# A spectral filter and a squared-ReLU MLP in one kernel: first part reordered, one residual by matmul, two column stages ahead in the drain, bias adds moved

## The chip, the cores and the metric

The kernel runs on one core of a Trainium2 chip. The core has five instruction queues that run side by side[...]: TensorE (PE, matrix multiplies, which write PSUM), VectorE (DVE), ScalarE (ACT), GpSimd (POOL) and SyncE (SP, which issues loads and stores). The metric is device time in microseconds (us) of one launch. A chunk of work is faster only if the last instruction of the program ends earlier, so what matters is who waits for whom.

## The reference, cut to what matters

Both halves work on x of 2048 rows and 512 columns, in bf16, and both have a residual.

```python
h  = x + irfft2(rfft2(layernorm(x)) * (w_r + 1j * w_i))     # w: 2048 x 257
u  = layernorm(h)
a  = relu(u @ w1 + b1) ** 2                                 # w1: 512 x 1792
out = h + a @ w2 + b2                                       # w2: 1792 x 512
```

The Fourier transforms are done as matrix products with tables of sines and cosines. The layernorm has no gain or bias; its mean only touches one frequency column, so the first part needs just the reciprocal standard deviation of each row.

## The kernel before, in words

**Layout.** Row 16p + g of x lies in partition p, group g, so there are 16 groups of 128 rows (tile xs).

**First part (to L315).** Pool makes index tables by iota and memset (L136 to L157). DVE turns them into angles (L159 to L178): fiE[0] (L168) for the table EF of the row transform, fiK (L172, L174) for the table KF. ACT takes sines of them (L191 to L194). Pool makes fiE[1] (L179) and the angles fiG of the column transform (`angles_g`, L181). Meanwhile each group's variance is found: bn_stats and bn_aggr on DVE (`ln1_stats`, L204), for groups 3, 7 and 11 two activations with sums on ACT (`ln1_sums`, L197). Pool turns a variance into the reciprocal deviation rs1 with an add and a power (`ln1_rstd`, L215), and DVE scales the table KF by it into KFr (`ln1_fold`, L219). `stage1` (L223) then multiplies two groups of x by KFr on PE, eight matmuls of 256 columns, and copies the result to Bt. With split=True the two halves of the result lie in two PSUM tiles, and ACT and DVE copy one each. `warm` (L248) issues filler matmuls on a tile of ones, which compute nothing that is used.

SP's queue issues the loads in this order: five pieces of x, then the two filter arrays w_r and w_i (WB, L102), W1, W2, b1, b2 (L103 to L106). Two gathers with reversed row order (`w_reversed`, L148) are issued by Pool (L300, L301). ident, the identity matrix for transposes, is made by Pool (L296, L297).

**Middle (L318 to L470).** The spectrum is worked on in eight pairs of row frequencies, pr = 0 to 7. `stage2` is the column transform (PE, then a copy to U), `stage3` the row transform (PE, then a copy to X, or to AB with a butterfly on DVE for odd pr), `spectral` (L390) the filter on DVE: two products mA and mB, their combination Z, and M, the sums and differences of Z that the next stage takes. `stage4` (L413) is the inverse row transform: PE, then a copy to T2. The inverse tables EI and KI are transposes of EF and KF (`transposed`, L253; `table_i`, L260; `table_neg`, L265). The loop at L448 issues, in each turn, stage2 of pr + 3, stage3 of pr + 2, stage4 of pr - 1 and spectral of pr. All stages draw PSUM from four tiles of two banks. The sine of the last table GI is taken at pr = 4 (L467), the table of the square root is loaded at pr = 8 (L470).

**Drain (L660 to L674).** `s5` is the inverse column transform of one group: four matmuls, and a copy od of one half by ACT. `s5b` makes the sum and difference R on DVE. `s6` multiplies by KI and adds the residual x on DVE, giving hs. `s6b` gives mean and variance, either by two activations on ACT or by bn_stats on DVE. `rstd`, `norm` and `transp` give the normalised, transposed input UT of the MLP. In the drain this is done for chunk 0 (groups 0 and 1); nothing else can run on PE meanwhile, so `warm` fills it.

**MLP (L588 on).** The 16 groups go in chunks of 2, 3, 4, 4 and 3. For each chunk come 14 up slots (four matmuls into ph, a ReLU on ACT into rl, a square on DVE into act) and, for each group, three down slots (5, 5 and 4 matmuls into po), then the output: DVE adds hb, which is hs + b2, made on Pool (L605), and SP stores it. The column stages of the next chunk are placed between these slots by `prep_steps` (L564) and `run` (L645): each step has a due time in estimated PE time, and is issued after the slot at which the running sum of estimates (0.22 us for each matmul of 512 columns, 0.44 for an s5, 0.12 for each group of a transpose step) has reached it. What is still left is issued after the last slot. PSUM has 3 banks for pp, 3 for ph, 2 for po.

At the end `pin` (L22) fixes the program order of each engine as it was written. Semaphore waits and the reuse of buffers follow from the data.

The order of the first part, as it stands before, in short:

```python
    ln1_stats(0, 1); ln1_rstd(0, 2); angles_g(0)
    ln1_stats(2, 4, 5); ln1_fold(0, 2); stage1(0, 8)
    ln1_rstd(2, 6); angles_g(1)
    ln1_stats(6, 8, 9); ln1_fold(2, 6); stage1(2)
```

Of the kernel before, what the change touches and what calls it, by code (L numbers as in the profile page):

```python
# [15 lines left out]
P = 128  # L16
# [18 lines left out]
def kernel(  # L35
# [38 lines left out]
    ident = persist.tile([P, P], BF16, name="ident")  # L74
    mhalf = persist.tile([P, 4], FP32, name="mhalf")
# [9 lines left out]
    WB = [fwd.tile([P, 23, Df], BF16, name=f"WB{i}") for i in range(2)]  # L85
# [5 lines left out]
    Cn = fwd.tile([P, len(ON_PE), P], BF16, name="Cn")  # L91
    KFr = fwd.tile([P, G, 256], BF16, name="KFr")
# [4 lines left out]

    CH = ((0, 2), (2, 4), (4, 8), (8, 12), (12, 16))
    for a, b in CH:
        nc.sync.dma_start(xs[:, a:b, :], xv[:, a:b, :])  # L100
    for i in range(2):
        nc.sync.dma_start(WB[i][:, 0:16, :], wvs[i])  # L102
    nc.sync.dma_start(W1[:], B_w1.rearrange("(c p) f -> p c f", p=P))  # L103
    nc.sync.dma_start(W2[:], B_w2.rearrange("(i p) d -> p i d", p=P))
    nc.sync.dma_start(b1b[:], B_b1.rearrange("(i p) -> p i", p=P))
    nc.sync.dma_start(b2b[:], B_b2.unsqueeze(0).to_broadcast([P, D]))  # L106
# [37 lines left out]
    nc.gpsimd.iota(subc[:], pattern=[[0, 16], [1, 8]], base=0, channel_multiplier=0)  # L144
    nc.gpsimd.iota(idxR[:], pattern=[[0, 1]], base=(P - 1) * 16 * 257, channel_multiplier=-16 * 257)
    nc.gpsimd.memset(ones[:], 1.0)  # L146

    def w_reversed(i):  # L148
        nc.gpsimd.indirect_dma_start(
            out=WB[i][:, 16:23, :].rearrange("p j l -> p (j l)"), out_offset=None,  # L150
            in_=(A_w_r, A_w_i)[i].rearrange("k l -> (k l)").unsqueeze(1), element_offset=9 * Df,
            in_offset=bass.IndirectOffsetOnAxis(ap=idxR[:, 0:1], axis=0))
# [4 lines left out]
    nc.gpsimd.memset(eps[:], EPS)  # L157

# [15 lines left out]
    nc.vector.scalar_tensor_tensor(fiK[:], subc[:].rearrange("p q s -> p (q s)"), pF[:, 2:3], fiK[:],  # L174
                                   ALU.is_equal, ALU.mult)

    nc.vector.tensor_scalar(cols[:, 0:1], pF[:, 0:1], 128.0, None, ALU.mult)
    nc.vector.tensor_scalar(cols[:, 1:2], pF[:, 0:1], 128.0, 16384.0, ALU.mult, ALU.add)  # L178
    nc.gpsimd.tensor_scalar(fiE[1][:], fiE[0][:], 1.0, float(QT), ALU.mult, ALU.add)  # L179
# [14 lines left out]
    table_e(1)  # L194
# [28 lines left out]
    def stage1(g0, n=0, split=False, cp=nc.scalar.copy):  # L223
# [7 lines left out]
        warm(pts[0], n)  # L231
        for t in range(2):
# [8 lines left out]
        if split:  # L241
            for t, cp in ((0, nc.scalar.copy), (1, nc.vector.tensor_copy)):
                cp(dst[:, 2 * t:2 * t + 2], pts[t].rearrange("p (e i q s) -> p e i q s", e=2, i=2, q=16))
            return two[0][:, 512:1024].bitcast(BF16)
        else:
            cp(dst, pt[:].rearrange("p (e i q s) -> p e i q s", e=4, i=2, q=16))
# [21 lines left out]
    for g in (3, 7, 11):  # L268
        ln1_sums(g)
    ln1_stats(0, 1)  # L270
    ln1_rstd(0, 2)
    angles_g(0)
    ln1_stats(2, 4, 5)
    ln1_fold(0, 2)
    stage1(0, 8)
    ln1_rstd(2, 6)
    angles_g(1)
    ln1_stats(6, 8, 9)
    ln1_fold(2, 6)
    stage1(2)  # L280
    ln1_rstd(6, 10)
    stage1(4)
    ln1_stats(10, 12)
    ln1_rstd(10, 12)
    ln1_fold(6, 10)
    stage1(6)
    ln1_stats(13)
    ln1_fold(10, 12)
    ln1_rstd(12, 14)
    sin_of(GF[:].rearrange("p t c -> p (t c)"), fiG[:])  # L290
    stage1(8)
    ln1_stats(14, 15)
    ln1_rstd(14, 16)
    ln1_fold(12, 14)
    stage1(10, cp=nc.vector.tensor_copy)
    nc.gpsimd.memset(ident[:], 0.0)  # L296
    nc.gpsimd.affine_select(out=ident[:], in_=ident[:], compare_op=ALU.not_equal,  # L297
                            fill=1.0, base=0, pattern=[[-1, P]], channel_multiplier=1)
    ln1_fold(14, 16)
    w_reversed(0)  # L300
    w_reversed(1)  # L301
    stage1(12, split=True)
    tr08 = stage1(14, split=True)
# [3 lines left out]
    nc.vector.tensor_scalar(Cn[:], EF[:, ON_PE[0]:ON_PE[-1] + 1:ON_PE[1] - ON_PE[0], 1, :], -1.0, None, ALU.mult)  # L307
    transposed(tr08, (0, 8), True)
# [7 lines left out]


# [3 lines left out]
    def stage2(pr, split=False):  # L321
        Us[pr] = U = fwd.tile([P, 2, 512], BF16, tag="U", bufs=3, name="U")
        if split:
            pus = [mm_tile(f"p2{q}")[:, 0:512] for q in range(2)]
        else:
            pu = mm_tile("p2")
            pus = [pu[:, 0:512], pu[:, 512:1024]]
        for q in range(2):
            puv = pus[q].rearrange("p (r e j) -> p r e j", r=2, e=2)
            for e in range(2):  # L330
                for t in range(2):
                    nc.tensor.matmul(puv[:, :, e, :], lhsT=Bt[:, 2 * t + 1 - e, 2 * pr + q, :], rhs=GFv[:, t, :, e, :],  # L332
                                     start=(t == 0), stop=(t == 1))
        Uv = U[:].rearrange("p q (r j e) -> p (q r) j e", r=2, e=2)
        if split:
            for q, cp in ((0, nc.scalar.copy), (1, nc.vector.tensor_copy)):
                cp(Uv[:, 2 * q:2 * q + 2], pus[q].rearrange("p (r e j) -> p r j e", r=2, e=2))
        else:
            nc.scalar.copy(Uv, pu[:].rearrange("p (q r e j) -> p (q r) j e", q=2, r=2, e=2))  # L339
# [49 lines left out]
    def spectral(pr):  # L389
# [4 lines left out]
        step = 23 - 2 * pr if pr else 8  # L394
# [3 lines left out]
        Ms[pr] = M = fwd.tile([P, 2, 2, 256], BF16, tag="M", bufs=2, name="M")  # L398
        ABs.pop(pr, None)
        nxt[0]()  # L400
        nc.vector.tensor_tensor(Z[:, :, 0], mA[:, :, 0], mB[:, :, 1], ALU.subtract)
        nc.vector.tensor_tensor(Z[:, :, 1], mA[:, :, 1], mB[:, :, 0], ALU.add)
        nxt[1]()
        if pr == 0:
            nc.vector.tensor_scalar(M[:, :, 0], Z[:, :, 1], -1.0, None, ALU.mult)
            nc.vector.tensor_copy(M[:, :, 1], Z[:, :, 0])
        else:
# [5 lines left out]
    def stage4(pr, split=False):  # L413
        Z, M = Zs.pop(pr), Ms.pop(pr)
        pts = [mm_tile("p4a"), mm_tile("p4b")] if split else [mm_tile("p4")] * 2
        for lt in (1, 0, 3, 2):
            r, e = lt // 2, lt % 2
            pt = pts[r]
            if pr == 0:
                for u, k1 in ((0, 0), (1, 8)):  # L420
                    o = pt[:, 256 * lt + P * u:256 * lt + P * u + P]
                    nc.tensor.matmul(o, lhsT=Z[:, u, r, e::2], rhs=EI[:, k1, 1, :], start=True, stop=False)
                    nc.tensor.matmul(o, lhsT=M[:, u, r, e::2], rhs=EI[:, k1, 0, :], start=False, stop=True)
            else:
                o = pt[:, 256 * lt:256 * lt + 256]
                ei = EI[:, pr].rearrange("p k b -> p (k b)")
# [10 lines left out]
    stage2(0, split=True)  # L437
    stage2(1)
    stage3(0)
    nc.scalar.copy(KI[:], tr08[:, 4 * P:5 * P])  # L440
    table_i(tr08, (0, 8))
# [6 lines left out]
    for pr in range(9):  # L448
        if pr + 3 < 8:
            stage2(pr + 3)  # L450
        if 0 < pr and pr + 2 < 8:
            stage3(pr + 2)
        if pr > 0:
            stage4(pr - 1, split=(pr == 8))
        if pr >= 5:
            warm(mm_tile("idle")[:, 0:512], 5)
        if pr < 8:
            spectral(pr)
        if pr == 0:
            table_neg((1, 3))  # L460
# [29 lines left out]
    def s5(g):  # L490
        pe = bank("p5", "pp", 3)
# [5 lines left out]
        od = ffn.tile([P, 256], FP32, tag="od", bufs=3, name="od")  # L497
# [9 lines left out]
    def s6(g):  # L507
        py = bank("p6", "pp", 3)
        nc.tensor.matmul(py[:], lhsT=KI[:], rhs=Rs.pop(g)[:], start=True, stop=True)  # L509
        nc.vector.scalar_tensor_tensor(hs[:, g, :], py[:], WSC, xs[:, g, :], ALU.mult, ALU.add)  # L510
# [16 lines left out]
    def rstd(c):  # L527
        a, b = CHUNKS[c]
        for par in range(2):
            mine = [g for g in range(a, b) if on_act(c, g) != bool(par)]  # L530
            if mine:
                st = mine[1] - mine[0] if len(mine) > 1 else 1
                sl = slice(mine[0], mine[-1] + 1, st)
                nc.scalar.activation(sd2[:, sl], mv2[:, sl, 1], ACT.Sqrt, bias=eps[:], scale=1.0 if par else 1.0 / D)
# [29 lines left out]
    def prep_steps(c, total):  # L564
# [3 lines left out]
        t0 = 0.3 if c == 1 else total - 0.5 - 2.0 * n - 7.0  # L568
# [139 lines left out]
```

## Time and profile before

| | us |
|---|---|
| median of 4 runs | 179.16 (178.15 to 179.37) |
| the profiled execution | 178.93 |
| its span, first to last instruction | 177.1 |
| granted TensorE clock, mean | 0.979 of full |
| PE busy | 161.7 (91%) |
| DVE busy | 129.1 (73%) |
| ACT busy | 105.9 (60%) |
| POOL busy | 37.0 (21%) |

All times of instructions below are from the start of the span. L12 is line 12 of the kernel before. The first part lasts to about 21.7, the middle to 53.7 (the first s5), the drain to 61.0 (the first matmul of the MLP), the first MLP chunk to 76.9, the other four to 174.0, where the last output is added and stored. A busy PE counts matmuls whose ends are modelled, so the distance between the starts of two matmuls says more than their length. In the chain of waits each row is what the end of the program depended on at that moment.

### The profile page before, as it was taken

Reading aid. Unit: us, or ns where it says so; the run is one execution under the profiler, and the core shown is the slowest. Engines: PE = TensorE matmul, PEld = TensorE weight load, DVE = VectorE, ACT = ScalarE, POOL = GpSimd, SP = SyncE. Lnnn points to the kernel's source line nnn. Section 1 sums busy time; section 2 is a strip of 40 time slices with the busy share of each in tenths; the row PEclk is TensorE's granted clock in tenths of the full one; section 3 lists DMA queues with packets and bytes.
Section 4 is the critical chain, followed back from the end, with each engine's and each line's share of the span. In section 5 each row is a group of like instructions: output and inputs, shape, how many; then the busy total and the mean of one; then the engine's idle time right before and its main releaser. Section 6 shows DMA issues by size and latency. Waiting matters only on the chain.

```text
span 177.1 us, 2715 instructions
## 1 busy us (share of the span) xinstructions
PE 161.7 (91%) x984; PEld 93.0 (52%) x984; DVE 129.1 (73%) x300; ACT 105.9 (60%) x184; POOL 37.0 (21%) x62
## 2 busy tenths in 40 slices
PE   3479898999888899999999999999999999999992
PEld 1157566777453576466544544544544454455461
DVE  6999779799976479869889466579756648468321
ACT  3976677998845586059753488454278623568300
POOL 7585841000000050006100053100025200025000
PEclk9956999999999999999999999999999999999999
DMA  5999992000000000010000100000100000110011
GB/s 148 331 408 417 359 319 41 0 4 2 0 0 0 4 2 0 0 61 4 0 0 31 60 1 0 2 30 30 33 30 0 0 30 0 33 61 0 0 40 48
DMA packets 7917, 11.19 MB, mean 63 GB/s; under 512 B 2272, under 2 KB 6368, under 8 KB 7648
## 3 DMA queue, kind: packets, MB, share of 16 engines
q1 hardware_dynamic: 7744, 10.11, 16.8%
q0 software_dynamic: 160, 0.92, 1.6%
q8 instruction: 7, 0.11, 0.3%
q14 instruction: 6, 0.05, 0.1%
HBM read 8.93 MB, written 2.10 MB: 62 GB/s over the span
## 4 chain that ended last, share of the span: by engine, by line
PE 62%; DVE 24%; ACT 8%; issue 3%; POOL 0%; DVEq 0%; POOLq 0%; ACTq 0%
PE ph L598 26%; PE po L631 20%; DVE st L210 3%; PE p L495 3%; ACT U L339 2%; PE p L556 2%; DVE hs L510 2%; PE p L236 2%; PE p L238 2%; PE p L509 2%; ACT junk L517 2%; PE po L619 2%; DVE mB L396 2%; DVE mA L396 2%; DVE act L602 2%
## 5 line engine op out<-in xcount | busy, mean ns | idle before, releaser
L598 PE MATMUL ph<-UT,W 128*128 128x384 bf16 (+2 forms) x280 | 50.3, 336 | 0.5 <-ACT UT L560 0.5
L601 ACT ACTIVATE rl<-ph,b1f 128x384 bf16<-128x384 f32 (+2 forms) x70 | 41.7, 602 | 12.9 <-PE ph L598 10.3
L631 PE MATMUL po<-W,act 128*128 128x512 bf16 x210 | 49.2, 379 | 0.0
L602 DVE TENSOR_TENSOR act<-rl 128x384 bf16<-128x384 bf16 (+2 forms) x70 | 35.1, 530 | 15.3 <-ACT rl L601 15.0
L605 POOL TENSOR_TENSOR hb<-hs,b2b 128x512 f32<-128x512 bf16 x16 | 18.5, 1156 | 114.7 <-DVE act L602 81.2
L598 PEld LDWEIGHTS <-W 128*128 128x128 bf16 x280 | 27.4, 98 | 22.1 <-issue 1.0
L631 PEld LDWEIGHTS <-act 128*128 128x128 bf16 x210 | 20.3, 98 | 21.7 <-issue 0.8
L635 DVE TENSOR_TENSOR ot<-po,hb 128x512 bf16<-128x512 f32 x15 | 10.3, 689 | 9.3 <-PE po L631 8.0
L510 DVE SCALAR_TENSOR_TENSOR hs<-p,xs 128x512 bf16<-128x512 f32 x16 | 10.8, 682 | 1.9 <-PE p L509 1.9
L236 PE MATMUL p<-KFr,xs 128*128 128x256 bf16 x24 | 8.0, 354 | 3.6 <-DVE KFr L221 3.6
L498 ACT COPY od<-p 128x256 f32<-128x256 f32 x16 | 5.9, 371 | 8.4 <-PE p L495 8.4
L560 ACT COPY UT<-p 128x768 bf16<-128x768 bf16 (+2 forms) x5 | 4.2, 841 | 10.3 <-PE p L556 10.3
L517 ACT ACTIVATE junk<-hs 128x512 bf16<-128x512 bf16 x7 | 4.4, 629 | 9.4 <-DVE hs L510 9.4
L495 PE MATMUL p<-GI,T 128*128 128x256 bf16 x64 | 9.4, 272 | 0.1
L251 PE MATMUL idle<-ones 128*128 128x512 bf16 x37 | 9.0, 379 | 0.0
L251 PEld LDWEIGHTS <-ones 128*128 128x128 bf16 x45 | 4.7, 106 | 7.8 <-POOL ones L146 2.9
L495 PEld LDWEIGHTS <-T 128*128 128x128 bf16 x64 | 6.2, 98 | 4.3 <-issue 1.8
L210 DVE BATCH_NORM_STATS2 st<-xs 128x6 f32<-128x512 bf16 x13 | 8.3, 673 | 0.0
L504 DVE TENSOR_TENSOR R<-p,od 128x256 bf16<-128x256 f32 x16 | 6.6, 415 | 2.3 <-ACT od L498 2.3
L332 PE MATMUL p<-GF,Bt 128*128 128x256 bf16 x64 | 8.3, 273 | 0.0
L435 ACT CAST T<-p 128x1024 bf16<-128x1024 f32 x7 | 7.1, 1033 | 1.8 <-PE p L428 1.8
L238 PE MATMUL p<-KFr,xs 128*128 128x256 bf16 x24 | 8.1, 356 | 0.0
(155 smaller groups left out, 230.0 us busy)
## 6 DMA issues: line engine op xcount, KB each, us to landing
W<-in_B_w_dram SPq DMA_DIRECT2D x2, 1792.0 KB, 18.3
out_dram<-ot SPq DMA_DIRECT2D x15, 128.0 KB, 1.8
xs<-in_A_x_dram SPq DMA_DIRECT2D x3, 512.0 KB, 7.2
WB<-in_A_w_r_dram SPq DMA_DIRECT2D x1, 1028.0 KB, 9.9
WB<-in_A_w_i_dram SPq DMA_DIRECT2D x1, 1028.0 KB, 11.4
xs<-in_A_x_dram SPq DMA_DIRECT2D x2, 256.0 KB, 3.4
b2b<-in_B_b_dram SPq DMA_DIRECT2D x1, 128.0 KB, 11.0
out_dram<-ot SPq DMA_DIRECT2D x2, 64.0 KB, 1.5
```

Of the source, the lines that this page charges most:

```text
L210: nc.vector.bn_stats(st[:], xs[:, g, :])
L236: nc.tensor.matmul(o, lhsT=xs[:, g, P * t:P * t + P], rhs=KFr[:, g, 0:P].unsqueeze(1).to_broadcast([P, 2, P]), start=True, stop=False)
L238: nc.tensor.matmul(o, lhsT=xs[:, g, 256 + P * t:256 + P * t + P], rhs=KFr[:, g, :].rearrange("p (e c) -> p e c", e=2), start=False, stop=True)
L251: nc.tensor.matmul(o, lhsT=ones[:, 0:P], rhs=ones[:], start=True, stop=True)
L495: nc.tensor.matmul(pe[:, 256 - 256 * e:512 - 256 * e], lhsT=T2[:, lt, g].rearrange("p q s -> p (q s)"), rhs=GI[:, lt, :], start=(r == 0), ...
L510: nc.vector.scalar_tensor_tensor(hs[:, g, :], py[:], WSC, xs[:, g, :], ALU.mult, ALU.add)
L598: nc.tensor.matmul(ph[:, 0:n], lhsT=W1[:, d, bass.ts(f, P)], rhs=UT[:, d, 0:n], start=(d == 0), stop=(d == ND - 1))
L601: nc.scalar.activation(rl[:, 0:n], ph[:, 0:n], ACT.Relu, bias=b1f[:, f:f + 1], scale=1.0)
L602: sq = nc.vector.tensor_tensor(act[:, f, 0:n], rl[:, 0:n], rl[:, 0:n], ALU.mult)
L605: add = nc.gpsimd.tensor_tensor(hb[:, g, :], hs[:, g, :], b2b[:], ALU.add)
L631: nc.tensor.matmul(po[:], lhsT=act[:, f, bass.ts(i, P)], rhs=W2[:, f, :], start=(f == 0), stop=(f == NF - 1))
L635: nc.vector.tensor_tensor(ot[:], po[:], hb[:, g, :], ALU.add)
```

## The change

It has four parts.

1. **First part.** SP: the load of groups 8 to 11 waits for the first load, the first filter load for the third; the filter loads take 9 rows of each partition's 16, since the other 7 come only through the gathers (WB has 16 rows instead of 23). The loads of W1, W2, b1, b2 are issued after both gathers have landed. Pool: the two scalars of L177 and L178 move from DVE to Pool, fiE[1] from before the first statistics to after the first power, the first angles wait for fiK, the first gather comes ahead of the power for groups 6 to 9, the second ahead of ident, and a second scaled identity (identW) is made. ACT: table_e(1) comes after stage1(4). DVE: statistics of 5 and 9 come later, the add before the last power is on DVE. stage1(10) is split between ACT and DVE. stage1(0) has 14 fillers instead of 8, stage1(2) has 4 and stage1(6) has 3. The five transposes for EI and KI go ahead of stage1(14).
2. **Middle.** stage2 of pairs 0 and 1 is issued in halves around stage3(0). The copies to EI (first part) and KI move from ACT to DVE. M is no longer made for pairs 0, 5 and 6: stage4 takes Z alone, with 16 matmuls instead of 8 for pairs 5 and 6 and a negated table EN. The transposes of EI 4 to 7 move from pair 0 to pair 1, their negation to pair 3, the sine of GI to pair 5, the square-root table to pair 6. The fillers (five in each of four turns) become three in turn 7 and three in turn 8. In the last stage4 the matmuls with the first half of M come before those with the second.
3. **Drain.** The column stage s5 of groups 2 and 3 is issued right after that of 0 and 1, into the po banks, and s5b(2) after norm(0); three fillers leave. For group 0 the residual is added in PSUM by a matmul of identW with x, and one ACT activation writes hs and its sum. A second gives the sum of squares; the scales in `rstd` follow from that.
4. **MLP.** The bias adds on Pool for chunk 0 come after its last square. `prep_steps` starts from step 2 for chunk 1, and its steps are due 0.3 earlier, except for the transposes.

```diff
 CH = ((0, 2), (2, 4), (4, 8), (8, 12), (12, 16))
+ld = []
 for a, b in CH:
-    nc.sync.dma_start(xs[:, a:b, :], xv[:, a:b, :])
+    ld.append(nc.sync.dma_start(xs[:, a:b, :], xv[:, a:b, :]))
+after(ld[3], ld[0], "the first rows first")
 for i in range(2):
-    nc.sync.dma_start(WB[i][:, 0:16, :], wvs[i])
-nc.sync.dma_start(W1[:], B_w1.rearrange("(c p) f -> p c f", p=P))
-nc.sync.dma_start(W2[:], B_w2.rearrange("(i p) d -> p i d", p=P))
-nc.sync.dma_start(b1b[:], B_b1.rearrange("(i p) -> p i", p=P))
-nc.sync.dma_start(b2b[:], B_b2.unsqueeze(0).to_broadcast([P, D]))
+    w = nc.sync.dma_start(WB[i][:, 0:9, :], wvs[i][:, 0:9, :])
+    if i == 0:
+        after(w, ld[2], "the rows of x first")
...
+nc.gpsimd.memset(identW[:], 0.0)
+nc.gpsimd.affine_select(out=identW[:], in_=identW[:], compare_op=ALU.not_equal,
+                        fill=1.0 / WSC, base=0, pattern=[[-1, P]], channel_multiplier=1)
...
-nc.vector.tensor_scalar(cols[:, 0:1], pF[:, 0:1], 128.0, None, ALU.mult)
-nc.vector.tensor_scalar(cols[:, 1:2], pF[:, 0:1], 128.0, 16384.0, ALU.mult, ALU.add)
-nc.gpsimd.tensor_scalar(fiE[1][:], fiE[0][:], 1.0, float(QT), ALU.mult, ALU.add)
+nc.gpsimd.tensor_scalar(cols[:, 0:1], pF[:, 0:1], 128.0, None, ALU.mult)
+nc.gpsimd.tensor_scalar(cols[:, 1:2], pF[:, 0:1], 128.0, 16384.0, ALU.mult, ALU.add)
...
-table_e(1)
...
 ln1_stats(0, 1)
+after(nc.gpsimd.tensor_scalar(fiG[:, 0:256], idxL[:, 0:256], cols[:, 0:1], float(QT), ALU.mult, ALU.add), fk,
+      "the angles of the first stage first")
+nc.gpsimd.tensor_scalar(fiG[:, 256:512], idxL[:, 256:512], cols[:, 0:1], float(HT), ALU.mult, ALU.add)
 ln1_rstd(0, 2)
-angles_g(0)
-ln1_stats(2, 4, 5)
+nc.gpsimd.tensor_scalar(fiE[1][:], fiE[0][:], 1.0, float(QT), ALU.mult, ALU.add)
+ln1_stats(2, 4)
 ln1_fold(0, 2)
-stage1(0, 8)
+stage1(0, 14)
+ln1_stats(5)
 ln1_rstd(2, 6)
-angles_g(1)
-ln1_stats(6, 8, 9)
+ln1_stats(6, 8)
 ln1_fold(2, 6)
-stage1(2)
+gathers = [w_reversed(0)]
+stage1(2, 4)
+stage1(4)
+table_e(1)
+ln1_stats(9)
 ln1_rstd(6, 10)
-stage1(4)
 ln1_stats(10, 12)
 ln1_rstd(10, 12)
+angles_g(1)
 ln1_fold(6, 10)
-stage1(6)
+stage1(6, 3)
 ln1_stats(13)
-ln1_fold(10, 12)
 ln1_rstd(12, 14)
 sin_of(GF[:].rearrange("p t c -> p (t c)"), fiG[:])
+ln1_fold(10, 12)
 stage1(8)
 ln1_stats(14, 15)
-ln1_rstd(14, 16)
+nc.vector.tensor_scalar(rs1[:, 14:16], mv1[:, 14:16, 1], EPS, None, ALU.add)
+nc.gpsimd.tensor_tensor(rs1[:, 14:16], rs1[:, 14:16], mhalf[:, 0:2], ALU.pow)
 ln1_fold(12, 14)
-stage1(10, cp=nc.vector.tensor_copy)
+gathers.append(w_reversed(1))
 nc.gpsimd.memset(ident[:], 0.0)
 nc.gpsimd.affine_select(out=ident[:], in_=ident[:], compare_op=ALU.not_equal,
                         fill=1.0, base=0, pattern=[[-1, P]], channel_multiplier=1)
+stage1(10, split=True)
 ln1_fold(14, 16)
-w_reversed(0)
-w_reversed(1)
+for k, (dst, src) in enumerate(((W1[:], B_w1.rearrange("(c p) f -> p c f", p=P)),
+                                (W2[:], B_w2.rearrange("(i p) d -> p i d", p=P)),
+                                (b1b[:], B_b1.rearrange("(i p) -> p i", p=P)),
+                                (b2b[:], B_b2.unsqueeze(0).to_broadcast([P, D])))):
+    load = nc.sync.dma_start(dst, src)
+    if k == 0:
+        for ga in gathers:
+            after(load, ga, "the rows of W first")
 stage1(12, split=True)
-tr08 = stage1(14, split=True)
...
-nc.vector.tensor_scalar(Cn[:], EF[:, ON_PE[0]:ON_PE[-1] + 1:ON_PE[1] - ON_PE[0], 1, :], -1.0, None, ALU.mult)
-transposed(tr08, (0, 8), True)
+tr08 = stage1(14, split=True, pre=lambda o: transposed(o, (0, 8), True))
...
-stage2(0, split=True)
-stage2(1)
+stage2_one(0, 0, nc.scalar.copy)
+stage2_one(0, 1, nc.vector.tensor_copy)
+stage2_one(1, 0, nc.scalar.copy)
+nc.vector.tensor_copy(EI[:, 0::8, 0:2, :], tr08[:, 0:4 * P].rearrange("p (a k b) -> p a k b", a=2, k=2))
+cos_negs()
 stage3(0)
-nc.scalar.copy(KI[:], tr08[:, 4 * P:5 * P])
-table_i(tr08, (0, 8))
+stage2_one(1, 1, nc.scalar.copy)
 stage3(1)
...
+def stage2_one(pr, q, cp):
+    o = mm_tile(f"p2{q}")[:, 0:512]
+    stage2_half(pr, q, o)
+    cp(Us[pr][:, q].rearrange("p (r j e) -> p r j e", r=2, e=2), o.rearrange("p (r e j) -> p r j e", r=2, e=2))
...
+    if pr > 0 and pr not in NO_M:
+        Ms[pr] = M = fwd.tile([P, 2, 2, 256], BF16, tag="M", bufs=2, name="M")
...
+        if M is None:
+            en = EN[:, NO_M.index(pr), :]
+            mms = [(u, r, ei[:, P:3 * P]) for u in range(2)]
+            mms += [(u, 1 - r, en if u == r else ei[:, 0:2 * P]) for u in range(2)]
+            for k, (u, c, tb) in enumerate(mms):
+                nc.tensor.matmul(o, lhsT=Z[:, u, c, e::2], rhs=tb, start=(k == 0), stop=(k == 3))
...
+    if pr == 7:
+        warm(mm_tile("idle")[:, 0:512], 3)
     if pr > 0:
         stage4(pr - 1, split=(pr == 8))
-    if pr >= 5:
-        warm(mm_tile("idle")[:, 0:512], 5)
-    if pr < 8:
+    if pr == 8:
+        warm(mm_tile("idle")[:, 0:512], 3)
+    if pr == 1:
+        table_neg((1, 3))
+    if pr == 3:
+        table_neg((4, 7))
+        nc.vector.tensor_scalar(EN[:].rearrange("p n (k b) -> p n k b", k=2), EI[:, NO_M[0]:NO_M[-1] + 1, 0:2, :],
+                                -1.0, None, ALU.mult)
+    if pr == 0:
+        spectral(0, first_tables)
+    elif pr < 8:
         spectral(pr)
-    if pr == 0:
-        table_neg((1, 3))
+    if pr == 1:
         tr = mm_tile("ptr", BF16)
         transposed(tr, (4, 5, 6, 7))
         table_i(tr, (4, 5, 6, 7))
-    if pr == 1:
-        table_neg((4, 7))
-    if pr == 4:
+    if pr == 5:
         sin_of(GI[:].rearrange("p t c -> p (t c)"), fiI[:])
         nc.gpsimd.tensor_copy(b1f[:], b1b[:])
-    if pr == 8:
+    if pr == 6:
         nc.scalar.activation(junk1[:], eps[:], ACT.Sqrt, bias=eps[:])
...
 def s6(g):
     py = bank("p6", "pp", 3)
+    if g == 0:
+        nc.tensor.matmul(py[:], lhsT=identW[:], rhs=xs[:, 0, :], start=True, stop=False)
+        nc.tensor.matmul(py[:], lhsT=KI[:], rhs=Rs.pop(g)[:], start=False, stop=True)
+        nc.scalar.activation(hs[:, 0, :], py[:], ACT.Copy, scale=WSC, accum_out=mv2[:, 0, 0:1])
+        return
...
-t0 = 0.3 if c == 1 else total - 0.5 - 2.0 * n - 7.0
-gap = (total - 7.0 - t0) / (n + 1)
+first = 2 if c == 1 else 0
+end = total - 7.3
+t0 = 1.2 if c == 1 else total - 0.5 - 2.0 * n - 7.0
+gap = (end - t0) / (n + 1 - first)
+t0 = end - (n + 1) * gap
...
-if f % 3 == 1 and f // 3 < b - a:
-    g = a + f // 3
+mine = [a + f // 3] if c and f % 3 == 1 and f // 3 < b - a else range(a, b) if not c and f == NF - 1 else []
+for g in mine:
...
 s5(0)
 s5(1)
+s5(2, True)
+s5(3, True)
-warm(idle[:], 3)
 s5b(0)
 s5b(1)
 s6(0)
...
-warm(idle[:], 14)
+warm(idle[:], 12)
+s5b(2)
 transp(0, 0)
```

## The prediction

> **What bounds the kernel now.** I read the chain of waits in order of time first, because the change touches only the first 77 us, then busy time by stage, then the instructions of Pool, DVE and ACT around each place. Stages, by the table of stretches (us, then PE, PEld, DVE, ACT, POOL busy, granted PE clock, DMA share, GB/s):
>
> ```profile
> 9.34:12.75 3.41, 2.66 (x14) 1.67 (x13) 3.41 (x12) 2.82 (x7) 3.06 (x6) 0.50 1.00 422
> ...
> 16.00:21.70 5.70, 4.82 (x43) 3.65 (x41) 4.20 (x12) 4.25 (x6) 4.30 (x9) 0.99 1.06 378
> 21.70:34.40 12.70, 11.66 (x106) 8.96 (x105) 9.93 (x24) 10.05 (x14) 3.10 (x7) 1.00 0.51 138
> 34.40:51.60 17.20, 16.13 (x113) 10.69 (x111) 16.73 (x40) 14.02 (x15) 0.00 (x0) 1.00 0.01 1
> 61.00:76.90 15.90, 15.36 (x112) 10.28 (x112) 13.01 (x36) 8.23 (x19) 2.37 (x2) 1.00 0.01 2
> 76.90:174.00 97.10, 96.08 (x534) 50.00 (x532) 64.74 (x132) 52.93 (x100) 16.12 (x14) 1.00 0.07 22
> ```
>
> From 34.4 to 51.6 DVE is full (16.73 of 17.2); from 76.9 on PE is (96.08 of 97.1), and nothing of the change can shorten that part. The first stage has DVE full, PE at half clock, DMA saturated. The chain (start, us, what) gives the owner of each moment:
>
> ```profile
> 18.41 1.22 DVE Bt L246
> ...
> 23.65 1.01 ACT U L339
> ...
> 52.55 1.09 PE idle L251 x5
> ...
> 56.25 0.61 DVE hs L510
> 56.88 0.73 ACT junk L517 x2
> 57.63 0.82 ACT junk L517 x2
> 58.48 0.49 ACT sd L534 x2
> ...
> 63.89 1.22 DVE act L602 x2
> ```
>
> So: a DVE copy holds the last fold (18.4), ACT holds 23.7 to 34.4, five filler matmuls hold the first matmul of the drain, and two squares take 1.22 us because of Pool. Pool's instructions in order of time show what the diff permutes:
>
> ```profile
> 4.01 1.18 POOL L179 TENSOR_SCALAR fiE<-fiE 128x1152 int32<-128x1152 int32 x1 [0.54 <-DVE fiE L168]
> ...
> 18.90 1.23 POOL L149 DMA_INDIRECT WB<-in_A_w_r_dram,idxR  x1 [0.20 <-issue]
> 20.43 0.95 POOL L149 DMA_INDIRECT WB<-in_A_w_i_dram,idxR  x1 [0.31 <-issue]
> ...
> 63.54 1.22 POOL L605 TENSOR_TENSOR hb<-hs,b2b 128x512 f32<-128x512 bf16 x1 [33.42 <-PE ph L598]
> ```
>
> [...]L174 takes 1.04 us under Pool's L179 where its sibling L172 takes 0.34, and a square takes over 0.9 us under L605 where the first takes 0.29. A fold L221 under Pool's L184 took 0.31 against 0.25, so folds are not blocked. [...]the window 5.93 to 9.34, PE 15% busy, was followed by half clock; the next, 78% busy, did not lift it; a full one did, at 16.1. Between 15% and 67% (the least in a window that kept its clock) nothing is shown. [...]the load at 52.75 takes 1.28.
>
> **First part (to stage 2, T0 = 21.7).** Moving fiE[1] off L174 saves 0.7 us of DVE, moving the two column scalars (L177, L178) to Pool 0.1: the first bn_stats starts at 4.65, not 5.45, and x is there (first landing 2.8 us after issue at 0.74). identW's two Pool instructions (0.5) lie in Pool's gap before fiE[1]. Fourteen fillers end at 7.45 (seven at 0.43 apart, seven at 0.216 once the clock is up, as at 5.9), before the first fold. One stats less before the first fold: it ends at 7.9, not 9.31 (0.66 of that is the postponed one). From there DVE meets Pool. Pool's chain for folds 6 to 9 is now pow, first gather (1.23), add, pow: gather 10.25 to 11.5, rs at 13.2, folds 13.3 to 14.15 against 13.55 to 14.39. The lead has shrunk to 0.24. Stats 14, 15 end at 16.75 (16.98 before), pow at 17.65 (18.18). The full DVE copy of stage1(10) (1.22) becomes half a copy (0.7, the row of L243), so the last fold ends at 18.5, not 20.14. But the ident for the five transposes, now ahead of stage1(14) on PE's queue, comes behind the second gather on Pool: 17.65, gather to 19.0, two ident instructions (0.56 in the trace) to 19.7 or 19.85. Stage1(14) starts at 20.2 (19.89 before), its DVE half copy ends near 21.95 (21.75). Moved transposes save PE 0.35 us, under that copy's wait, so nothing. On SP, the load of rows 8 to 11 waits for the first load (near 3.6) and W for the third; behind them stand only loads, and ACT and DVE want rows 8 to 11 from 8.6 on, with 2.1 MB at 345 to 410 GB/s in by about 8.6: nothing, or 0.5 if late. PE at full clock or half hardly matters up to 16 us, since DVE's folds come last. Sum: +0.2, from -0.4 (gathers of 0.95, no gaps) to what the clock rival gives.
> DMAs: 9 rows of each W instead of 16 leave 2.1 + 1.2 MB ahead of the gathers; W1 and W2 are held on SP until the second gather lands, so near 21 to 24, and their 3.6 MB at the 410 GB/s seen need 9 us, against a first use at 61. b1b and b2b stand behind them on SP (b1b took 22 us to land): about 45, first use at 61 too. Hidden; uncovered it would cost only if over 15 us later.
>
> **Middle (T0 to the first s5).** Relative to T0: X(0) gets ready 0.3 earlier since stage2 of pair 1 is cut in two around stage3(0), but its second half of U is now copied after X, so AB(1) is 0.5 later. M of pair 0 (0.4) is saved ahead of a DVE wait for ACT: nothing. KI and EI leave ACT (0.66 in its chain), EI of 4 to 7 (about 0.95) goes behind pair 3, so ACT delivers AB(3) at 34.3 as before (34.4). From there DVE runs on: M of pairs 5 and 6 gone, 44.70 to 45.46 and 47.93 to 48.68, -1.5; EN and the negation of 4 to 7 now inside this stretch, two of 0.29 (row L266), pitch 0.25: +0.5. The eight added matmuls of stage4(5) and stage4(6), 8 x 0.109 each, fall where the fillers of 5 x 0.216 stood: nothing. After M(7) the trace has 2.1 us to the first s5 (51.55 to 53.68): three fillers instead of five -0.43; the first half of M used before the second, -0.27. ACT now carries EI, GI and the table load (1.28 + 0.29) ahead of its last copies; if they end 0.3 late, that is paid. Sum: -1.5 + 0.5 - 0.7 + 0.3 = -1.4; bounds -0.4 (ACT is the bound) and -1.8.
>
> **Drain (53.68 to 61.0).** Group 0 goes hs (DVE 0.61) then Copy (0.73) then Square (0.82); with the residual in PSUM the Copy writes hs: -0.61 there. But group 1 still needs DVE: its hs at +3.03 after the first s5 instead of +3.16, its aggregate at +4.65 instead of +4.71. Gain: this 0.05 and one square root of 0.24 no longer in line: -0.3. The od copies of groups 2, 3 (2 x 0.38) on ACT end at +2.3, just as the Copy may start: nothing; the scaling of one column and s5b(2) lie beside ACT and PE: nothing; 0 to -0.5. The residual matmul (0.216) runs while PE waits for R.
>
> **First MLP chunk (61.0 to 76.9).** In the trace starts lie 0.109 us apart at 256 columns, 0.216 at 512, 0.056 at 128. PE's own work before: 56 x 0.109 + 3 x 0.436 + 3 x 0.216 + 28 x 0.216 + 12 x 0.056 = 14.8 of 15.87. Two s5 leave: -0.87. The Pool adds come after the last square, so the 0.9 us of PE waits that the squares caused shrink to about 0.15: -0.75. Against it, the planner: after the slot "second group, 5 to 10" its clock reads 12.54, and the transposes are due at 12.62 (before: 13.42, so they ran, and the last four down matmuls covered the UT copies). They now come last, and PE waits for the copy: 0.34 + 0.2 + 0.8 from their start, less 0.67 of transposes: +0.7. Sum -0.9; the bias adds end near +12, before the second output needs them at +13.4; if they block DVE, +0.3. Bounds -1.5 and -0.3.
> Later chunks: steps due 0.3 earlier; one (the last s6 of chunk 4) moves ahead by a slot, where PE waits 0.6 for R, and loses a wait of 0.6 at 154: 0.
>
> **Sum.** +0.2 - 1.4 - 0.3 - 0.9 = -2.4. The profiled execution was 178.93 (span 177.1 and 1.8 around it), 0.23 under the median of the runs, 179.16. Profile 176.5, runs **176.7**.
>
> **Rivals.** A measurement of this kernel tells about 0.5% (0.9 us) from no change.
> 1. ACT bounds the middle and the chunk gains half: -0.4 - 0.6 - 0.2 + 0.2 = -1.0: 178.1. For it: ACT has 14.0 of 17.2 and gets 1.0 more; against: its idle at 47.9 to 49.7.
> 2. Clock: PE idles from 18.2 to 19.9, so a window from 16.2 to 19.6 would be 30% busy, in the unknown band. Half clock for the next 6.8 us doubles stage1(14), three quarters of stage2 and stage3(0): +2.7: 179.4. For: the 15% window; against: 67% kept it, and the phase may differ.
> 3. Slower: Pool's gathers are starved. [...]They now lie among bn_stats and folds. [...]It decides from 2.9 us a gather. Against: 1.23 under DVE work in the trace.
> 4. All better: early gathers short and ident in time, middle at its bound: -3.6: 175.5.
>
> **Chances.** Forecast 0.45, rival 1 0.18, rival 2 0.13, rival 3 0.12, rival 4 0.12. Faster by over 0.5%: 0.45 + 0.12 + 0.13 + 0.02 = 0.72; within: 0.05 + 0.08 + 0.02 = 0.15; slower: 0.03 + 0.10 = 0.13. The range leaves out half of rival 3 and the ends of 4: 174.8 to 180.2; the forecast's own is 175.6 to 177.6.
>
> **What would show it.** L174 near 0.35; first bn_stats at 4.6; stage1(14) waiting for ident near 19.8; granted clock in 16 to 26; DVE full from 34 to M(7), 1.0 sooner after T0; first s5 1.4 sooner; drain of 7.0; chunk 0 of 15.0 with 0.7 of PE waiting for UT at its end; 97 us after. Gathers over 2 us, half clock after 19.6, or ACT full before the drain make it wrong.

## The result and the profile after

The changed kernel takes 178.67 us (median of 35 runs, 177.46 to 180.21), the kernel before, run beside it, 178.73 us (56 runs, 177.88 to 179.58). The ratio is 0.998 with a 95% interval of 0.996 to 1.000. The forecast was 176.7 us, a gain of 1.3%, and that gain did not come. The time lies inside the range, 174.8 to 180.2.

The runs of the changed kernel are not spread evenly. For 37 of them, the profiled one included, the mean granted TensorE clock is on record, and it sorts them: 16 at full clock, 15 of them at 177.46 to 177.49 us and one at 177.89; 13 at a clock of 0.99, at 178.62 to 179.00; 8 at 0.98, at 179.88 to 180.21. The profiled execution, 179.94 us with a span of 178.2, is of the last kind. The median falls into the middle group, so the result poses two questions: why the first group stands at 177.5 and not at 176.7, and what puts the other runs 1.2 and 2.5 us above it.

Busy time by stretch of the changed kernel, cut at the same events as the stretches shown of before (us, then PE, PEld, DVE, ACT, POOL busy, granted PE clock, DMA share, GB/s):

```profile
16.30:24.31 8.01, 4.97 (x33) 3.21 (x32) 5.08 (x15) 3.99 (x6) 6.16 (x14) 0.76 0.20 61
24.31:37.94 13.63, 12.08 (x94) 8.59 (x95) 9.19 (x22) 8.88 (x12) 0.20 (x1) 0.89 0.93 279
37.94:54.20 16.26, 15.91 (x130) 12.22 (x128) 15.79 (x38) 15.55 (x18) 0.00 (x0) 1.00 0.01 2
62.99:78.00 15.01, 14.23 (x104) 9.60 (x104) 11.93 (x35) 7.46 (x17) 2.26 (x2) 1.00 0.03 9
78.00:175.00 97.00, 95.59 (x533) 49.96 (x532) 64.20 (x131) 53.09 (x100) 16.12 (x14) 1.00 0.06 21
```

What was forecast from 38 us on is there: the stretch with DVE full is 16.26 us long instead of 17.14, the first MLP chunk 15.01 instead of 15.87, the rest 97.0 as before. But stage 2, which should begin near 21.95, begins at 24.31, and the clock in the two stretches around it is 0.76 and 0.89. The chain of waits at that place, and at the drain and the end of the first chunk (start, us, what):

```profile
18.24 0.69 POOL rs L312
18.93 0.18 issue
19.11 1.10 POOL WB L157
20.22 0.23 POOL ident L315
20.52 0.57 POOL ident L316
21.13 0.58 PE p1a L267 x4
...
23.56 0.70 DVE Bt L254
24.31 2.52 PE p L352 x11
...
55.92 0.61 PE p L555 x4
...
62.99 0.61 PE ph L672 x4
...
77.14 0.81 ACT UT L631
78.00 2.11 PE ph L672 x12
```

Before, this place belonged to a DVE copy (L246) and a fold. Now it belongs to Pool: power, second gather, ident, and then the transposes that stand in front of stage1(14). The same place, instruction by instruction:

```profile
18.00 0.17 DVE L311 TENSOR_SCALAR rs<-mv 128x2 f32<-128x2 f32 x1
19.11 1.10 POOL L157 DMA_INDIRECT WB<-in_A_w_i_dram,idxR  x1 [0.18 <-issue]
19.52 0.27 PE L249 MATMUL p1b<-KFr,xs 128*128 128x256 bf16 x1
20.50 0.49 DVE L331 TENSOR_SCALAR EF<-EF 128x1152 bf16<-128x1152 bf16 x1
20.52 0.56 POOL L316 TENSOR_SCALAR_AFFINE_SELECT ident<-ident 128x128 bf16<-128x128 bf16 x1
21.13 0.58 PE L267 MATMUL p1a<-ident,EF 128*128 128x128 bf16 x4 [1.33 <-POOL ident L316]
21.61 0.42 PE L247 MATMUL p1a<-KFr,xs 128*128 128x256 bf16 x1
23.56 0.69 DVE L254 CAST Bt<-p1b 128x512 bf16<-128x512 f32 x1 [2.57 <-PE p1b L249]
```

PE has nothing to do for 1.33 us while it waits for ident. After that its matmuls of 256 columns start 0.21 us apart and not 0.109: the clock is at half. The stretches of 3.4 us around the change of clock (columns as above):

```profile
17.03:20.43 3.40, 1.63 (x12) 0.94 (x11) 3.10 (x11) 2.67 (x4) 2.55 (x4) 1.00 0.00 0
20.43:23.83 3.40, 2.61 (x14) 1.62 (x13) 0.83 (x4) 0.59 (x1) 3.05 (x9) 0.50 0.45 140
23.83:27.26 3.43, 2.95 (x13) 1.90 (x14) 1.66 (x4) 0.97 (x2) 0.00 (x0) 0.50 0.80 241
27.26:30.66 3.40, 2.94 (x23) 2.00 (x21) 2.56 (x6) 2.10 (x4) 0.00 (x0) 1.00 1.03 402
```

The recorded clock falls to 0.50 at 20.43 and reads 1.00 again from 27.26, 6.83 us later, as long as it was at half in the kernel before (9.32 to 16.14). In the 3.40 us before the fall PE was busy for 1.63, which is 48%. One more thing differs from the forecast, further up in the queues of Pool and DVE:

```profile
7.29 1.15 POOL L286 TENSOR_SCALAR fiE<-fiE 128x1152 int32<-128x1152 int32 x1
7.37 1.33 DVE L230 TENSOR_SCALAR KFr<-KF,rs 128x256 bf16<-128x256 bf16 x2
8.62 0.68 DVE L219 BATCH_NORM_STATS2 st<-xs 128x6 f32<-128x512 bf16 x1
```

The first two folds should take 0.25 us each. They take 1.33 together in this profile, where Pool began its 1152-wide addition 0.08 us before them, and the next statistics come behind them. The profile has no wait ahead of the first fold: the instruction itself lasts 1.15 us, from 7.37 to 8.52, and ends 0.08 us after the addition.

### The profile page after: what moved, and what is told of

Same layout as the page of the kernel before. It is cut to its first block, busy times and chain, and to the rows that moved or that the text cites. A ratio compares the mean times of both kernels' runs of the same rounds, so it can differ in the third digit from the quotient of the medians.

```text
span 178.2 us, 2735 instructions
## 1 busy us (share of the span) xinstructions
PE 161.6 (91%) x995; PEld 94.1 (53%) x995; DVE 126.9 (71%) x297; ACT 106.2 (60%) x184; POOL 37.0 (21%) x65
## 4 chain that ended last, share of the span: by engine, by line
PE 65%; DVE 18%; ACT 7%; POOL 5%; issue 3%; POOLq 0%; ACTq 0%; DVEq 0%
PE ph L672 26%; PE po L705 23%; PE p L555 2%; DVE st L219 2%; PE p L352 2%; DVE KFr L230 2%; PE p L574 2%; DVE hs L575 2%; PE p L627 2%; PE po L693 2%; ACT U L368 2%; POOL rs L226 2%; ACT rl L675 1%; DVE R L564 1%; DVE R L565 1%
## 5 line engine op out<-in xcount | busy, mean ns | idle before, releaser
L676 DVE TENSOR_TENSOR act<-rl 128x384 bf16<-128x384 bf16 (+2 forms) x70 | 34.2, 513 | 16.3 <-ACT rl L675 15.8
L705 PEld LDWEIGHTS <-act 128*128 128x128 bf16 x210 | 20.4, 98 | 21.7 <-issue 0.6
L575 DVE SCALAR_TENSOR_TENSOR hs<-p,xs 128x512 bf16<-128x512 f32 x15 | 10.3, 683 | 2.4 <-PE p L574 2.4
L352 PE MATMUL p<-GF,Bt 128*128 128x256 bf16 x64 | 9.6, 299 | 0.6 <-DVE Bt L254 0.6
L262 PE MATMUL p<-ones 128*128 128x512 bf16 x21 | 6.9, 489 | 2.9 <-POOL ones L153 2.9
L586 ACT ACTIVATE junk<-hs 128x512 bf16<-128x512 bf16 x6 | 3.8, 632 | 7.6 <-DVE hs L575 7.6
L262 PEld LDWEIGHTS <-ones 128*128 128x128 bf16 x39 | 4.2, 110 | 7.7 <-POOL ones L153 2.9
L352 PEld LDWEIGHTS <-Bt 128*128 128x128 bf16 x64 | 6.6, 105 | 2.5 <-DVE Bt L254 0.9
L574 PE MATMUL p<-R,KI 128*128 128x512 bf16 x15 | 5.7, 381 | 1.6 <-DVE R L565 1.6
```

Source lines behind the costliest of these rows:

```text
L262: nc.tensor.matmul(o, lhsT=ones[:, 0:P], rhs=ones[:], start=True, stop=True)
L676: sq = nc.vector.tensor_tensor(act[:, f, 0:n], rl[:, 0:n], rl[:, 0:n], ALU.mult)
L705: nc.tensor.matmul(po[:], lhsT=act[:, f, bass.ts(i, P)], rhs=W2[:, f, :], start=(f == 0), stop=(f == NF - 1))
```

## The experiments

The theory after the traces is that middle, drain and first chunk gain what they should, and that the first part gives it back in three ways: ident behind the second gather, the clock that PE loses while it waits for ident, and the addition over the first folds. The main rival: the middle was never bound by DVE, so the gain is not there at all. All kernels below compute the whole result.

**Old first part, new rest; new first part, old rest.** The first kernel takes the changed one and puts back the loads, the Pool order, the folds and stage 1 of before, with its transposes behind stage1(14); the second is its complement, the kernel before with the lines of the change that stand ahead of the middle.

```diff
 # old first part, new rest
-    gathers = [w_reversed(0)]
-    tr08 = stage1(14, split=True, pre=lambda o: transposed(o, (0, 8), True))
+    w_reversed(0)
+    w_reversed(1)
+    tr08 = stage1(14, split=True)
+    transposed(tr08, (0, 8), True)
...
```

> The changed kernel with the first part of the kernel before (loads, Pool order, folds, stage 1, transposes after stage 1), the rest as changed. Theory (the middle, the drain and the first MLP chunk gain what they should, and the first part takes it back): stage 2 at 21.7, and 178.7 - 1.2 - 0.25 - 0.85 = 176.4 us. Rival (ScalarE bounds the middle, so that only drain and chunk gain): 177.6. Rival (nothing of it is on the path): 178.7.

Measured: 175.73 us (175.28 to 176.50), ratio to before 0.983 (0.979 to 0.986).

> The kernel before with the new first part alone (loads, Pool order, folds, transposes ahead of the last stage 1), its middle, drain and MLP as before. Theory: stage 2 starts 1.4 us later at full clock and up to 2.6 later at half clock, and nothing behind gives it back: 180.1 to 181.3 us, in steps as the runs of the changed kernel. Rival (the middle absorbs a late start): 178.7 to 179.3.

Measured: 180.43 us (five runs at 180.37 to 180.47, one of 182.90 at clock 0.98, above the expected 181.3), ratio 1.011 (1.006 to 1.016).

So the first kernel is 3.0 us faster than before, 0.4 more than the forecast's 2.6 for the rest, and the new first part costs 1.7 us even at full clock, where the forecast had 0.2. Together that is -1.3, from 178.7 to 177.4, which is where the runs at full clock lie. The rival that the middle has no gain is out: it asked for 177.6 in the first kernel.

Not all of the 3.0 need be the rest's own. In the profile of the first kernel the last copy of stage 1 ends at 21.20, in that of the kernel before at 21.75, though both have the same first part. In its chain of waits the last matmul row of 0.21 us starts at 15.09, in that of the kernel before at 15.90, and the latter shows why that counts:

```profile
11.38 0.26 DVE KFr L221
11.69 0.37 PE p L236
12.06 0.21 PE p L238
...
16.11 0.19 PE p L236
...
18.41 1.22 DVE Bt L246
```

From 11.69 to 16.1 the old first part waits for matmuls of stage 1 that start 0.21 us apart, at half clock, and the copy at 18.41 had waited 1.07 us for PE; in the first kernel it had waited 0.56 and starts at 17.95. Counted from the last copy of stage 1, the rest takes 152.6 us instead of 155.4, a gain of 2.8.

**Fillers in the wait for ident.** Seven matmuls on a tile of ones are put ahead of the transposes, later three (a 3 in place of the 7).

```diff
-    tr08 = stage1(14, split=True, pre=lambda o: transposed(o, (0, 8), True))
+    tr08 = stage1(14, 7, split=True, pre=lambda o: transposed(o, (0, 8), True))
```

> Seven filler matmuls (7 x 0.216 us) ahead of the five transposes, so that TensorE does not idle for 1.33 us while it waits for ident. Theory (the idle time halves the clock): clock 1.00 in every run, stage 2 starts at 23.2 us instead of 24.3, all runs near 177.5, none at 178.7 or 180.0; median 1.2 us below the changed kernel's 178.67. Rival (the clock falls for the gap at 17.5 to 18.5, or for another reason): runs stay spread over 177.5 to 180.2 with a median of 178.7.

Measured: 177.52 us, all six runs at 177.51 to 177.54, clock 0.997 to 1.000.

> The changed kernel itself once more, for a profile in which TensorE keeps its full clock after 19.6 us. Theory: runs at 177.5, 178.7 and 180.0 again; a profile of the first kind shows stage 2 from 23.2, the first s5 at 53.5, the first ph at 60.6 and the end as with the fillers (span 175.7), so that the fillers by themselves gain nothing but the clock. Rival (the three steps have another cause than the clock after 19.6): a run of 177.5 with half clock there, or one of 180.0 without.

Measured, the changed kernel once more: 177.53, 177.55 and 177.64 at clock 0.999 to 1.000, and one run of 180.24 at 0.98. No run at 178.7 this time, with only four runs. The profile is of the first kind:

```profile
21.14 0.38 PE L267 MATMUL p1a<-ident,EF 128*128 128x128 bf16 x4 [1.33 <-POOL ident L316]
23.24 1.38 PE L352 MATMUL p<-GF,Bt 128*128 128x256 bf16 x11 [0.26 <-DVE Bt L254]
53.51 1.91 PE L555 MATMUL p<-GI,T 128*128 128x256 bf16 x16 [0.23 <-DVE T L478]
60.57 1.47 PE L672 MATMUL ph<-UT,W 128*128 128x256 bf16 x12 [0.45 <-ACT UT L631]
75.58 2.60 PE L672 MATMUL ph<-UT,W 128*128 128x384 bf16 x15 [0.55 <-ACT UT L631]
```

The wait for ident is the same 1.33, but stage 2 starts at 23.24 and not at 24.31, the first s5 comes at 53.51 and not at 55.92, and the span is 175.7, the same as with seven fillers. So the fillers change nothing else; they only keep the clock. The 2.5 us between the two profiles are 1.07 before stage 2 and 1.34 in the middle, both ahead of 27.26, while the clock is at half.

> The changed kernel with three fillers (0.65 us) ahead of the transposes, where seven filled the whole wait for ident. Theory[...]: with 0.65 of it filled all or nearly all runs are at 177.5. Rival (any pause of over 0.6 us is enough): steps at 178.7 and 180.0 in a third or more of the runs.

Measured: 177.53 to 177.61 in four of four runs. With three fillers the least busy stretch of 3.4 us (taken every 0.5 us) has PE busy for 1.79, or 53%; without them it is 1.19, or 35%, and the stretch ahead of the fall in the first profile had 48%. Four runs could all be at full clock by luck at about 1 in 20, if 19 of 41 runs of the changed kernel are; so this is a hint that the busy share counts, and shows no limit.

A stretch of 3.4 us with less than 48% does not always cost the clock: in the full-clock profile of the changed kernel the one with 35% (17.5 to 20.9) lies within a clock of 1.00. The moments at which the traces record a change of the clock are 5.90, 9.32 and 16.14 in the kernel before, and 6.78, 20.43 and 27.26 in the changed one. They are 3.41, 6.83, 13.65 and 6.83 us apart, one, two, four and two times 3.41. Why one run of the changed kernel keeps its clock and another loses it, no run here shows.

**ident ahead of the second gather.**

```diff
-    gathers.append(w_reversed(1))
     nc.gpsimd.memset(ident[:], 0.0)
     nc.gpsimd.affine_select(out=ident[:], in_=ident[:], compare_op=ALU.not_equal, ...
+    gathers.append(w_reversed(1))
```

> The two instructions that make ident go ahead of the second gather on Pool. Theory (ident is what stage 1 of groups 14 and 15 waits for): ident ready at 19.8 instead of 21.1, PE idles 0.2 instead of 1.33, the clock stays at 1.00, stage 2 starts at 22.0 to 22.3 instead of 24.3, and the whole takes 176.3 to 176.6. The second gather then lands 0.9 later, with 10 us to spare. Rival (the middle absorbs an earlier start, because ScalarE or VectorE has a chain of its own): 177.4 or more.

Measured: 176.01 us, six runs at 175.99 to 176.01, ratio 0.984 (0.981 to 0.987), better than the 176.3 to 176.6 expected. Its instructions in order of time:

```profile
18.91 0.20 POOL L314 MEMSET ident<- 128x128 bf16 x1
19.19 0.33 POOL L315 TENSOR_SCALAR_AFFINE_SELECT ident<-ident 128x128 bf16<-128x128 bf16 x1
19.65 0.39 PE L267 MATMUL p1a<-ident,EF 128*128 128x128 bf16 x4
19.69 1.10 POOL L157 DMA_INDIRECT WB<-in_A_w_i_dram,idxR  x1 [0.18 <-issue]
21.75 1.37 PE L352 MATMUL p<-GF,Bt 128*128 128x256 bf16 x11 [0.26 <-DVE Bt L254]
```

The transposes no longer wait at all. Stage 2 starts at 21.75, 1.49 sooner than in the full-clock profile of the changed kernel, and the end comes 1.5 sooner too: nothing in the middle absorbs an earlier start. No run lost its clock; of the stretches from 16.5 to 23.4 the least busy has PE at 2.26 of 3.40, or 66%. One exchange of three lines on Pool thus turns the change from no gain into one of 2.7 us. Further experiments stand on this kernel, because its runs agree to 0.02 us.

**The addition over the first folds.** First fiE[1] goes behind the first gather, then it is held until the second fold is done.

```diff
     ln1_rstd(0, 2)
-    nc.gpsimd.tensor_scalar(fiE[1][:], fiE[0][:], 1.0, float(QT), ALU.mult, ALU.add)
     ln1_stats(2, 4)
     ln1_fold(0, 2)
+    after(nc.gpsimd.tensor_scalar(fiE[1][:], fiE[0][:], 1.0, float(QT), ALU.mult, ALU.add), folds[1], ...
```

> On top of the kernel with ident ahead of the second gather (176.01 us): the 1152-wide addition on Pool (fiE[1]) goes behind the first gather. Theory (it holds the first fold for 0.9 us and with it all of VectorE's first part): both first folds 0.25 us, then 0.9 sooner up to the first gather, but the addition then delays the powers for groups 6 to 9 by 0.6 of that: 175.7. Rival (the powers on Pool, not VectorE, set the last fold): 176.0.

Measured: 176.02 us, no gain. The two folds take 0.47 together, folds 2 to 5 come at 10.23 instead of 11.09, and then DVE waits 1.01 us for the power of groups 6 to 9, whose folds are again at 14.32: the addition now stands ahead of that power. The rival holds for this place.

> On top of the kernel with ident ahead of the second gather (176.01 us): fiE[1] is held until the second fold is done, so that it lies under three statistics instead of under a fold. Theory: first fold 0.25 instead of 1.15, the addition from 7.9 to 9.1, folds 2 to 5 at 10.4 instead of 11.1, and the last fold 0.65 sooner: 175.4. Rival (statistics are held by Pool as the fold was): no gain, 176.0.

Measured: 175.49 us (175.48 to 175.57), 0.52 sooner. Pool and DVE of this kernel:

```profile
7.94 1.16 POOL L290 TENSOR_SCALAR fiE<-fiE 128x1152 int32<-128x1152 int32 x1 [0.73 <-DVE KFr L232]
```

```profile
7.38 0.47 DVE L232 TENSOR_SCALAR KFr<-KF,rs 128x256 bf16<-128x256 bf16 x2
7.76 0.69 DVE L219 BATCH_NORM_STATS2 st<-xs 128x6 f32<-128x512 bf16 x1
10.57 0.87 DVE L232 TENSOR_SCALAR KFr<-KF,rs 128x256 bf16<-128x256 bf16 x4 [0.52 <-POOL rs L226]
```

The same addition over a statistics instruction leaves that at 0.69, against 0.68 elsewhere, and the two folds take 0.47 instead of 1.33. So in this kernel it matters which DVE instruction the addition lies over. Of the 0.9 us gained at the fold 0.5 reach the end, since the powers on Pool are next: folds 2 to 5 wait 0.52 for theirs.

**M of pairs 5 and 6 made again.**

```diff
-    NO_M = (5, 6)
+    NO_M = ()
```

> On top of the kernel with ident ahead of the second gather (176.01 us): M of pairs 5 and 6 is made by VectorE again (four of 0.34 us), the negated table EN (0.21) is left out, and stage 4 of these pairs has 8 matmuls fewer. Theory (VectorE is what bounds the middle from 34 us on): 4 x 0.34 - 0.21 = +1.1, 177.1. Rival (ScalarE's copies bound it): +0.3 at most, 176.3.

Measured: ten of 20 runs at 177.41 to 177.45 with full clock, 1.4 above the kernel it stands on; five at 178.68 to 178.83 (clock 0.99), five at 179.54 to 179.57 (0.98). The 1.4 agree with DVE as the bound (1.1 expected) and not with ACT (0.3). The steps come as a surprise: in the kernel it stands on, which has the same first part, no run loses its clock, so the place is probably another. With Z alone, stage 4 of a pair has eight more matmuls, and these keep PE busy near 49 us. Without them one stretch has PE at 36%, ahead of the drain (columns as above):

```profile
48.00:51.40 3.40, 1.22 (x8) 0.70 (x8) 3.26 (x9) 3.11 (x4) 0.00 (x0) 1.00 0.00 0
```

In the kernel it stands on, PE is busy for 3.00 of the same 3.40. That the clock is lost here is inferred: this profile is of a run at full clock.

**Transposes for chunk 1 due earlier.**

```diff
-        steps.append((total - 2.4, 0.12 * n, lambda: transp(c, 0)))
-        steps.append((total - 1.7, 0.12 * n, lambda: transp(c, 1)))
+        steps.append((total - (2.6 if c == 1 else 2.4), 0.12 * n, lambda: transp(c, 0)))
+        steps.append((total - (2.2 if c == 1 else 1.7), 0.12 * n, lambda: transp(c, 1)))
```

> On top of the kernel with ident ahead of the second gather (176.01 us): the two transposes for chunk 1 are due 0.2 and 0.5 earlier in the planner, so that the last four down matmuls of chunk 0 follow them. Theory (PE's wait of 0.55 for the ScalarE copy of UT is a cost of the planner's clock): the wait goes, 175.45 to 175.6. Rival (the transposes then wait for the layer norm instead): 176.0 or more.

Measured: 175.84 us, 0.17 sooner, between theory and rival. PE no longer waits for UT, but its transposes now spread over 1.38 us instead of 0.83. The rival, that they wait for the layer norm, explains most of it, as the last kernel below bears out. The last two kernels put the pieces together, the first with the edits of ident, of the second fold and of these transposes, the second with one more:

> The changed kernel with ident ahead of the second gather, fiE[1] held until the second fold is done, and the transposes for chunk 1 due earlier: the gains measured apart add up, 177.47 - 1.46 - 0.52 - 0.17 = 175.3 us. Rival (they share a wait): 175.5.

Measured: 175.35 us (175.35 to 175.36). The three gains add up.

> As the kernel before in this list, and the steps of chunk 1 that lead to its layer norm are due 0.6 us earlier, because the early transposes waited about 0.6 for the norm. Theory (the norm, not the transposes, is what is late): PE loses that wait too, 175.0 or a little less. Rival (the earlier residual matmul makes PE wait for R instead): 175.3 or more.

```diff
-        end = total - 7.3
+        end = total - (7.9 if c == 1 else 7.3)
```

Measured: 174.91 us (174.90 to 175.14), 0.44 less again, and 0.978 (0.976 to 0.980) of the kernel before. So the norm was what was late.

## Why the prediction was wrong, by its own steps

The sum can be checked term by term, with the full-clock profile of the changed kernel (span 175.7) against the profile before (span 177.1, at half clock from 9.3 to 16.1):

| step | forecast | measured | from |
|---|---|---|---|
| first part, start of stage 2 | +0.2 | +1.5 | 23.24 against 21.7 |
| middle, to the first s5 | -1.4 | -1.7 | 30.27 against 31.98 |
| drain | -0.3 | -0.26 | 7.06 against 7.32 |
| first MLP chunk | -0.9 | -0.86 | 15.01 against 15.87 |
| later | 0 | -0.1 | 100.1 against 100.2 |
| half clock | 0 | 0, +1.2 or +2.5 | groups of runs |

The profile at full clock is thus 1.0 us above the forecast (177.53 for 176.5): the first part cost 1.3 more, the rest gave 0.3 back. The median run adds 1.2 us of half clock, which the sum put at nothing.

- **"Folds are not blocked" is the first step that failed.** It was read from one fold under a 256-wide Pool instruction (0.31 against 0.25):

```profile
8.10 0.95 POOL L184 TENSOR_SCALAR fiG<-idxL,cols 128x256 int32<-128x256 int32 x2
8.82 0.49 DVE L221 TENSOR_SCALAR KFr<-KF,rs 128x256 bf16<-128x256 bf16 x2
```

The lines show a delay, though. Pool ends at 9.05 and the first fold, after its 0.31, at 9.13, 0.08 later, just as under the 1152-wide addition. This fold began 0.23 us before Pool's end; the one under the 1152-wide addition began 1.07 before it and took 1.15, and the pair 1.33 instead of 0.5. With the fold mended the end comes 0.5 sooner; the rest of the 1.2 us by which the last statistics ended late (17.96 for 16.75) is in the powers on Pool, which set folds 2 to 5 and 6 to 9.
- **The ident step failed in its size.** That ident comes behind the second gather, and that PE waits for it, was in the forecast, at 19.7 to 19.85. It came at 21.08: the whole delay of the statistics went through power, gather and ident without any slack, and the last instruction of ident took 0.56 instead of 0.29. It began 0.02 us after a tensor_scalar on DVE (L331, 0.49) and ended 0.09 after it. Whether that is the cause was not shown: in the kernel with ident ahead of the gather it lies over two folds on DVE and takes 0.33. Moving ident ahead of the gather gives 1.5 us, which is all that the first part cost at full clock.
- **The clock rival was right in its place and size**, and was given 0.13. Its stretch, 16.2 to 19.6 at 30% busy, was really 17.0 to 20.4 at 48%; its 6.8 us of half clock are 6.83; its +2.7 are +2.5 in 8 of 37 runs and +1.2 in 13 (half clock for about 3.5 us instead of 6.83, an estimate from the mean clock of 0.99 over a span of 176.9; no such run was profiled). What spoke against it, a clock kept at 67%, is 70% in the trace of before (24.36 to 27.77, the least busy 3.41 us ahead of the last output), so 48% was not covered by it. The mistake was to let it compete with the forecast as a case of its own. The wait for ident was part of the forecast, and so was the risk that it costs the clock: both grow with the same delay.
- **"PE at full clock or half hardly matters up to 16 us" failed too**, for the kernel before: its chain runs through PE at half clock from 11.69 on. With the same first part and the rows of 0.21 us over 0.8 us earlier, the last copy of stage 1 ended 0.5 us earlier. The forecast took DVE's folds to be last.
- **Gathers were not starved** (rival 3, whose size no trace of before shows): 1.22 and 1.10 us. Rival 1, ACT as the bound of the middle, is out: putting M back costs 1.4 us. But ACT is busy for 15.55 of 16.26 us there now (14.02 of 17.20 before), so a further cut on DVE may gain little; no run tried one.
- **The middle** gained 0.3 more than forecast. Stage 2 to the point where DVE runs full takes 12.28 instead of 12.71, where the forecast had no change (why, no run isolates); the full stretch, 35.52 to 51.86, is 0.8 shorter (forecast 1.0); from the last M to the first s5 it is 1.65 instead of 2.13 (forecast 0.4 less).
- **Right as they stood:** L174, now L185, at 0.35; first statistics at 4.57; 0.55 of waiting for UT at the end of the first chunk (forecast 0.7); the loads of W1 and W2, issued at 23.3 and landed 9.7 later; rows 8 to 11 late for ACT by 0.78, with no effect on the path.

## What to carry to other kernels

A reorder is only as good as its tightest chain. When a step is moved in front of the critical matmuls, follow everything it needs back through its own queue, add up the slack, and carry any delay found upstream through it; here the place of three lines on Pool decided 2.7 us. A pause of PE cost twice here, once as a wait of 1.33 us and once, in part of the runs, as half clock for the next 6.83 us (or about 3.5, by the estimate above). So runs in separate steps with different granted clocks are a sign to look for where the recorded clock falls, and for how busy PE is just ahead of it. When a Pool instruction must lie beside DVE work, compare the DVE instructions there with the same ones elsewhere: here one addition left statistics at 0.69 us and took two folds from 0.47 to 1.33.

## What the runs showed of the hardware

- Half clock came without an idle stretch. In the profiled run of the changed kernel PE was 48% busy in the 3.40 us ahead of it (17.03 to 20.43), in the kernel before 15% (5.93 to 9.34). The 48% is one stretch of one run, and one with 35% lay within a clock of 1.00 (full-clock profile of the changed kernel, 17.5 to 20.9), so no limit is shown. At half clock, stretches of 3.4 us with PE 78% busy (before, from 9.32) and 77% (changed, from 20.43) were followed by more half clock; one with 100% (before, from 12.73) and one with 86% (changed, from 23.85) were followed by full clock.
- One program has three times, 177.47, 178.7 and 180.0 us, at mean clocks of 1.00, 0.99 and 0.98. With the pause filled by seven matmuls, or gone, the six runs of each kernel agree to 0.03 us. Why runs of one program differ was not shown.
- A recorded clock of 1.00 was not full clock ahead of the first recorded change. In the changed kernel the profile reads 1.00 from 3.40 to 6.70, but fillers of 512 columns take 634 ns there and 380 from 6.95 on. In the kernel with the old first part it reads 1.00 from 9.3 to 12.7, but matmuls of 256 columns start 0.21 us apart from 12.10 on, against 0.11 at 17.75.
- Pool's 1152-wide tensor_scalar took 1.15 us over the two folds, which took 1.33 against 0.47 without it, and 1.16 over statistics, which took 0.69 against 0.68 elsewhere.
